# Loads of q for batch 0 are issued from ScalarE's queue instead of SyncE's

## The chip, the cores and the metric

The kernel runs on one core of one Trainium2 chip. A core has five engines that run their own instruction streams: TensorE (PE), VectorE (DVE), ScalarE (ACT), GpSimd (POOL) and SyncE (SP). In this kernel SP computes nothing and only issues transfers (DMAs). The metric is the device time of one execution in microseconds, as the median of several runs of the same program.

## What the kernel computes

Two parts follow each other for a batch of 4: a linear attention with 4 heads, 1088 positions and head size 32, and a gated feed-forward layer with a spatial (position by position) matrix. Cut to what matters:

```
a, b = S1 x, S2 x                      # 8 features each, phi(x) = all 64 products
kv = sum_s phi(k)_s v_s ;  z = sum_s phi(k)_s
attn = (phi(q) kv) / (phi(q) z + 1e-6)
h = gelu(attn @ w_in) ;  u, v = halves of h
v = layernorm(v) * g ;  v = w_sg @ v + b_sg      # w_sg is 1088 x 1088
out = attn + (u * v) @ w_out
```

## The kernel before

**Stages.** The work of batch 0's attention, the normalisation of its v and the first quarter of its spatial product are a stretch of their own, the head. From about 50 us on, a main loop runs: the spatial product of batch b on PE, and between its matmuls, small step by small step, the attention of batch b + 1. The loop's products are made of split operands (a high and a low part, the tiles with `_h` and `_l`), so each needs three matmuls.

**The head's order is written out.** `Head.build` names each step, with an engine, a length and what it comes after; a table of numbers, `HEAD`, gives each step a time, and `Steps.run` calls the steps in order of these times with the scheduler switched off. The engine that a step's entry names sorts nothing. The order in which the steps are called is the order in which each engine gets its instructions, and each engine works strictly in that order.

**The head's steps by name.** `s` is the raw projection (S1 and S2, repeated for the four heads: 128 rows, 16 KB). DVE makes `s_f` from it and from that the matrix `sk`; ACT makes eight scaled copies of `s_f`, `sab`. `k0` and `k1` load batch 0's k in two parts, 192 KB and 384 KB (128 rows of 384 and of 768 numbers). The steps `k1` on PE (line 755) multiply k by `sk` into three PSUM tiles `pk`: the first from the first part, the third and second from the other. ACT copies a piece of each, `kb` (line 764); DVE forms the features (line 146; they lie in the tile `vn`, which is named for what comes later in it). PE projects q with `sab` into `pab` (line 808), sums features times `vx` into `pkv` (line 776; `vx` is v), then forms `pnd` (numerators and denominators, line 847). DVE divides (lines 857 to 864, `den`, `xt`), PE transposes (`px`, line 873), ACT and DVE split the result into `x_h` and `x_l` (lines 876, 880). The raw weights `win_raw` are 64-bit numbers that DVE takes apart (lines 631 to 654) into `win_h`, `win_l`. The nine row blocks of the spatial matrix, `w_f`, 544 KB each, are loaded (line 707) and ACT rounds each to `w_h` (line 938).

**The loads.** `load_q(c)` loads batch 0's q in three tiles of 384 columns; the last is filled by two DMAs, as its rows end at 1088: 192, 192, 160 and 32 KB. All loads of the head are issued from SP, in this order: s, k0, k1, the four of q, the two halves of v, ident, the second half of w_in, then the blocks of `w_f` and the rest. A DMA completes on one of eight semaphores, which the program hands out in turn over all of its DMAs in the order in which their steps are called, whichever engine issues them; a DMA is not issued before the one that used the same semaphore before it has landed.

Before the head's first computed step ACT loads its table and runs one `warm` activation (line 113), and PE runs 14 small matmuls on constants (line 142).

Of the kernel before, what the change touches and what calls it, by code (L numbers as in the profile page):

```python
# [17 lines left out]
B, H, S, D, R = 4, 4, 1088, 32, 8  # L18
P = 128
NT = 9  # L20
SP = NT * P
# [67 lines left out]
def tile_kernel(ctx: ExitStack, tc: tile.TileContext, qd, kd, vd, sd, wd, bd, wind, gd, woutd, identd, outd):  # L89
    nc = tc.nc  # L90
    mm = nc.tensor.matmul
    V, A, G = nc.vector, nc.scalar, nc.gpsimd
    load = nc.sync.dma_start
# [59 lines left out]
    def spread(pool, ab, cw, name):  # L153

        d = dram.tile([2, 2, P, 3 * P], F32, tag="e", name=name + "d", bufs=3)
        load(
            d[0].rearrange("p (x j) c -> (p x) j c", j=R)[:, :, :cw],
            ab[:32, :cw].unsqueeze(1).broadcast_to([32, R, cw]),
        )
        for p in range(2):  # L160
            load(
                d[1, p].rearrange("(i x) c -> x i c", i=R)[:, :, :cw],
                ab[32 + 16 * p : 48 + 16 * p, :cw].unsqueeze(1).broadcast_to([16, R, cw]),
            )
        e = [pool([P, 2, 3 * P], "e" + x, name + x) for x in "ab"]
        for i in range(2):
            load(e[i][:, :, :cw], d[i].rearrange("p q c -> q p c")[:, :, :cw])
        return e
# [434 lines left out]
    class Head:  # L603
# [4 lines left out]
            self.pool, self.stage, self.x, self.g = pool, stage, x, g  # L608
            self.s = Steps()

        def load(self, name, ns, f, after=()):
            self.s.at(name, "SP", 0.47, f, after, late=-ns)

        def split64(self, name, hi, lo, raw, n, whole, after, late):

# [68 lines left out]
        def build(self):  # L684
# [5 lines left out]
            q = [pool([P, 512], "r", f"q0_{c}")[:, : 3 * P] for c in range(3)]  # L690
# [7 lines left out]
            def load_q(c):  # L698
                c0 = 3 * P * c
                n = min(3 * P, S - c0)  # L700
                load(q[c][:, :n], qd[0, :, c0 : c0 + n])
                if n < 3 * P:
                    load(q[c][:, n:], qd[0, :, S - (3 * P - n) : S])

            def load_w(t):
                w_f[t] = wpool([P, S], "w", f"w_f{t}")
# [3 lines left out]
            self.load("k0", 560, lambda: load(k[:, : 3 * P], kd[0, :, : 3 * P]))  # L710
            self.load("k1", 1460, lambda: load(k[:, 3 * P :], kd[0, :, 3 * P :]))
            self.load("q0", 550, lambda: load_q(0))
            self.load("q1", 550, lambda: load_q(1))
            self.load("q2", 700, lambda: load_q(2))
            self.load("v0", 760, lambda: load(vx[:, :NT], vd[0, :, 0]))
            self.load("v1", 760, lambda: load(vx[:, NT + 1 :], vd[0, :, 1]))
# [100 lines left out]
            for j in range(6):  # L817
                c, p = divmod(j, 2)
# [19 lines left out]
            n = 2 * (D + 1)  # L838
# [139 lines left out]
    late = Pool(gp, 3, gt=4)  # L978
# [114 lines left out]
```

## Time and profile before

| | us |
|---|---|
| median of 3 runs (lowest to highest) | 360.31 (360.22 to 360.52) |
| the profiled execution, its own time | 359.86 |
| its span, first to last instruction | 357.7 |
| busy: PE / DVE / ACT / POOL | 349.5 / 249.8 / 162.6 / 22.2 |
| the head, until the main loop's first matmul (line 390) | 0 to 50.42 |

The profile is that of one execution, 0.45 us below the median of the runs; 2.2 us of its time lie outside the span. A row of the timeline gives start, duration, engine, line, operation, output and inputs; in brackets the idle time of the engine ahead of it and what ended it. PE's durations overlap each other, since matmuls are pipelined; the distance between starts is what counts there. Where PE or DVE shows no bracket, it followed its previous instruction at once. For a DMA, the issue on the queue (SPq, ACTq) and the time from issue to landing are shown apart. TensorE's granted clock is 0.998 over the run.

### The profile page before, as it was taken

The page shows a single profiled execution, that of the slowest core. Times are in us where ns is not written, and L with a number is a line of the kernel's source. Part 1 is how long each engine was busy: PE and PEld are TensorE (multiplying, and loading weights), DVE is VectorE, ACT ScalarE, POOL GpSimd, SP SyncE. Part 2 cuts the span into 40 slices and gives each one's busy share as a digit, 9 for nine tenths or more (in the row PEclk, how much of TensorE's full clock was granted, in tenths as well). Part 3 has the DMA queues.
Part 4 walks back from the last instruction along what each step waited for, and adds up shares of the span by engine and source line. Part 5 has one row for each costly group of instructions (what it writes and reads, how often), then busy time and mean ns, then how long its engine had stood idle before and what let it go on. Part 6 is the DMA issues. An engine that isn't in the chain of part 4 may idle for free.

```text
span 357.7 us, 5455 instructions
## 1 busy us (share of the span) xinstructions
PE 349.5 (98%) x2024; PEld 321.2 (90%) x2024; DVE 249.8 (70%) x606; ACT 162.6 (45%) x355; POOL 22.2 (6%) x37
## 2 busy tenths in 40 slices
PE   8999999999999999999999999999999999999995
PEld 7876679998989999999898999999998899999994
DVE  5797899967999767627859765663696948642333
ACT  5475942325553963214546682332445595231210
POOL 0003000103010000022020000020202000000000
PEclk9999999999999999999999999999999999999999
DMA  7993005853400044483000007683000000100001
GB/s 227 394 412 134 2 0 98 237 174 66 123 21 2 0 103 128 149 222 138 2 0 23 1 0 160 132 206 88 2 0 1 2 0 23 41 0 2 0 2 62
DMA packets 18265, 30.18 MB, mean 84 GB/s; under 512 B 1984, under 2 KB 15168, under 8 KB 18240
## 3 DMA queue, kind: packets, MB, share of 16 engines
q1 hardware_dynamic: 18096, 29.77, 28.6%
q8 instruction: 16, 0.26, 0.3%
q10 hardware_dynamic: 144, 0.08, 0.1%
q14 instruction: 9, 0.07, 0.1%
HBM read 20.92 MB, written 8.91 MB: 83 GB/s over the span
## 4 chain that ended last, share of the span: by engine, by line
PE 82%; DVE 5%; ACT 5%; DMA 4%; POOL 1%; SPq 1%; issue 1%; DVEq 0%
PE pz L373 18%; PE pz L381 18%; PE pz L375 16%; PE pkv L202 3%; DMA w_f<-in_w 3%; ACT vn L345 2%; PE pu L390 2%; PE pz L932 2%; PE pv L297 2%; PE po L460 2%; PE pu L391 2%; PE pu L392 2%; PE po L458 2%; PE pv L298 2%; PE po L459 2%; PE pv L299 2%
## 5 line engine op out<-in xcount | busy, mean ns | idle before, releaser
L373 PE MATMUL pz<-w_h,vh 128*128 128x362 f32 (+3 forms) x405 | 133.6, 332 | 0.2 <-ACT vh L358 0.2
L381 PE MATMUL pz<-w_l,vh 128*128 128x362 f32 (+3 forms) x405 | 129.5, 329 | 0.0
L375 PE MATMUL pz<-w_h,vl 128*128 128x364 f32 (+3 forms) x360 | 118.2, 328 | 0.0
L373 PEld LDWEIGHTS pz<-w_h,vh 128*128 128x128 f32 x405 | 75.9, 188 | 2.0 <-ACT vh L358 1.0
L381 PEld LDWEIGHTS pz<-w_l,vh 128*128 128x128 f32 x405 | 75.5, 188 | 0.4
L375 PEld LDWEIGHTS pz<-w_h,vl 128*128 128x128 f32 x360 | 67.7, 188 | 1.2 <-DVE vl L363 0.4
L402 DVE SCALAR_TENSOR_TENSOR gt<-pz,g_col,b_bc 128x362 f32<-128x362 f32 (+3 forms) x47 | 27.5, 591 | 37.3 <-PE pz L381 36.8
L428 ACT CAST gh<-gt 128x362 fp32r<-128x362 f32 (+3 forms) x47 | 23.1, 497 | 57.9 <-PE po L459 47.6
L395 ACT ACTIVATE u<-pu 128x362 f32<-128x362 f32 (+3 forms) x48 | 22.6, 473 | 28.7 <-PE pu L392 27.3
L429 DVE TENSOR_TENSOR gl<-gt,gh 128x362 fp32r<-128x362 f32 (+3 forms) x47 | 24.6, 531 | 15.6 <-ACT gh L428 15.1
L345 ACT ACTIVATE vn<-vn,nm,rs 128x512 f32<-128x512 f32 x36 | 27.4, 811 | 6.3 <-POOL nm L679 3.9
L363 DVE TENSOR_TENSOR vl<-vn,vh 128x384 fp32r<-128x384 f32 (+2 forms) x60 | 23.0, 420 | 9.1 <-ACT vh L358 8.9
L425 DVE TENSOR_TENSOR gt<-gt,u 128x362 f32<-128x362 f32 (+3 forms) x47 | 25.2, 544 | 3.9 <-ACT u L395 3.5
L268 DVE RECIPROCAL den<-den 128x362 f32<-128x362 f32 (+1 forms) x9 | 21.8, 2417 | 8.7 <-ACT den L265 8.7
L358 ACT CAST vh<-vn 128x384 fp32r<-128x384 f32 (+1 forms) x63 | 23.0, 419 | 5.4 <-PE pz L381 5.4
L302 ACT ACTIVATE vn<-pv 128x512 f32<-128x512 f32 x27 | 15.9, 600 | 12.4 <-PE pv L299 12.1
L932 PE MATMUL pz<-w_f,vn 128*128 128x362 f32 (+3 forms) x54 | 18.0, 476 | 0.8 <-ACT vn L345 0.7
L305 DVE BATCH_NORM_STATS2 st<-vn 128x6 f32<-128x512 f32 x27 | 17.8, 676 | 0.6 <-ACT vn L302 0.5
L390 PE MATMUL pu<-x_h,win_h 128*128 128x362 f32 (+3 forms) x48 | 17.0, 354 | 0.2 <-ACT u L395 0.2
L460 PE MATMUL po<-gl,wout_h 128*128 128x362 f32 (+3 forms) x47 | 15.8, 336 | 0.9 <-DVE gl L429 0.9
L932 PEld LDWEIGHTS pz<-w_f,vn 128*128 128x128 f32 (+1 forms) x54 | 9.8, 189 | 7.6 <-ACT vn L345 2.4
L146 DVE TENSOR_TENSOR kp<-pk,kb 128x256 f32<-128x256 f32 x27 | 11.3, 422 | 7.1 <-ACT kb L190 4.4
(198 smaller groups left out, 525.6 us busy)
## 6 DMA issues: line engine op xcount, KB each, us to landing
w_f<-in_w SPq DMA_DIRECT2D x9, 544.0 KB, 9.8
vx<-in_v SPq DMA_DIRECT2D x8, 288.0 KB, 5.4
k<-in_k SPq DMA_DIRECT2D x3, 576.0 KB, 5.5
e_0d<-ab SPq DMA_DIRECT2D x3, 364.0 KB, 4.2
e_0d<-ab SPq DMA_DIRECT2D x6, 182.0 KB, 5.4
e_0a<-e_0d SPq DMA_DIRECT2D x3, 364.0 KB, 4.0
e_0b<-e_0d SPq DMA_DIRECT2D x3, 364.0 KB, 4.1
q<-in_q SPq DMA_DIRECT2D x6, 181.0 KB, 2.4
```

Of the source, the lines that this page charges most:

```text
L345: A.activation(self.vn[:, t], self.vn[:, t], AF.Identity, bias=self.nm[:, t : t + 1], scale=self.rs[:, t : t + 1])
L358: A.copy(vh[:, ts], vs[:, ts])
L363: self.last = V.tensor_sub(vl[:, ts], vs[:, ts], f32(vh[:, ts]))
L373: last = mm(z, lhsT=vh[:, t], rhs=w_h[:, t, cs], start=(t == 0), stop=False)
L375: last = mm(z, lhsT=vl[:, t], rhs=w_h[:, t, cs], start=False, stop=False)
L381: mm(z, lhsT=self.parts[db][0][:, t], rhs=w_l[t][:, c0 : c0 + cw], start=False, stop=(t == NT - 1))
L390: mm(pu, lhsT=win_h[:, ws], rhs=xh[:, cs], start=True, stop=False)
L402: V.scalar_tensor_tensor(gt, z, g_col[:, db : db + 1], b_bc[:, c0 : c0 + cw], op0=ALU.mult, op1=ALU.add)
L425: V.tensor_mul(gt, gt, u)
L428: A.copy(gh, gt)
L429: V.tensor_sub(gl, gt, f32(gh))
L932: return mm(zs[ci], lhsT=g.vn[r, t, :P], rhs=w_f[t][r, c0 : c0 + cw], start=(t == 0), stop=(t == NT - 1),)
```

## The change

`load_q` of the head issues its DMAs through `A.dma_start` (ACT's queue), where it used `load`, which is `nc.sync.dma_start`. `Head.load` gets an argument for the engine that a step's entry names; no call passes it.

```
-        def load(self, name, ns, f, after=()):
-            self.s.at(name, "SP", 0.47, f, after, late=-ns)
+        def load(self, name, ns, f, after=(), eng="SP"):
+            self.s.at(name, eng, 0.47, f, after, late=-ns)
...
             def load_q(c):
                 c0 = 3 * P * c
                 n = min(3 * P, S - c0)
-                load(q[c][:, :n], qd[0, :, c0 : c0 + n])
+                A.dma_start(q[c][:, :n], qd[0, :, c0 : c0 + n])
                 if n < 3 * P:
-                    load(q[c][:, n:], qd[0, :, S - (3 * P - n) : S])
+                    A.dma_start(q[c][:, n:], qd[0, :, S - (3 * P - n) : S])
```

The loads of q for batches 1 to 3 (line 223) stay on SP. Neither PE, DVE nor POOL gets another order of instructions. On ACT's queue at the start of the program, before:

```order
L113 ACT_TABLE_LOAD
L113 ACTIVATE warm<-eps_t 128x1 [waits DVE_49]
L743 ACTIVATE sab<-s_f,mask_67 128x8x8 [waits DVE_49]
L743 ACTIVATE sab<-s_f,mask_67 128x8x8 x4
L734 CAST sk_h<-sk 128x128 [waits DVE_49,Pool_49]
```

and now:

```order
L701 DMA q_0_138<-in_q 128x384
L113 ACT_TABLE_LOAD
L113 ACTIVATE warm<-eps_t 128x1 [waits DVE_49]
L701 DMA q_1_139<-in_q 128x384
L701 DMA q_2_140<-in_q 128x320
L703 DMA q_2_140<-in_q 128x64
L743 ACTIVATE sab<-s_f,mask_67 128x8x8 [waits DVE_49]
L743 ACTIVATE sab<-s_f,mask_67 128x8x8 x4
L734 CAST sk_h<-sk 128x128 [waits DVE_49,Pool_49]
```

The first load of q now stands ahead of ACT's table load, the other three between `warm` and `sab`. None of them waits. On SP's queue at the start, before:

```order
L709 DMA s_raw<-in_s 128x16
L710 DMA k_137<-in_k 128x384
L711 DMA k_137<-in_k 128x768
L701 DMA q_0_138<-in_q 128x384
L701 DMA q_1_139<-in_q 128x384
L701 DMA q_2_140<-in_q 128x320
L703 DMA q_2_140<-in_q 128x64
L715 DMA vx<-in_v 128x576
L716 DMA vx<-in_v 128x576 [waits DMAHW0_49]
L717 DMA ident<-in_ident 128x192 [waits DMAHW1_49]
L718 DMA win_raw_134<-in_w_in 128x512 [waits DMAHW2_49]
L707 DMA w_f_165<-in_w 128x1088 [waits DMAHW3_49]
```

and now:

```order
L709 DMA s_raw<-in_s 128x16
L710 DMA k_137<-in_k 128x384
L711 DMA k_137<-in_k 128x768
L715 DMA vx<-in_v 128x576
L716 DMA vx<-in_v 128x576 [waits DMAHW0_49]
L717 DMA ident<-in_ident 128x192 [waits DMAHW1_49]
L718 DMA win_raw_134<-in_w_in 128x512 [waits DMAHW2_49]
L707 DMA w_f_165<-in_w 128x1088 [waits DMAHW3_49]
```

All that stood behind q moves up by four issues. The waits carry the same names, but semaphore 0 is now that of q's first tile, 1 that of s, 2 and 3 those of k's two parts, 4 that of q's second tile, 5 that of the first half of v, 6 and 7 those of q's third: so the second half of v waits for q's first tile to land (before: for s), ident for s, `win_raw` for k's first part and the first `w_f` for its second.

## The prediction

> **What bounds the kernel now.** I read the page's table of engines first, then the chain that ended last, then the timeline of the first 21 us, then the transfers of that time in steps of half a microsecond.
>
> ```profile
> PE 349.5 (98%) x2024; PEld 321.2 (90%) x2024; DVE 249.8 (70%) x606; ACT 162.6 (45%) x355; POOL 22.2 (6%) x37
> 0.00:50.42 50.42, 48.19 (x241) 34.25 (x242) 39.69 (x123) 33.43 (x60) 3.58 (x18) 1.00 0.56 207
> 50.42:357.70 307.28, 301.29 (x1784) 286.95 (x1783) 210.16 (x484) 129.22 (x295) 18.63 (x19) 1.00 0.25 64
> ```
>
> The two lower rows are the busy times of PE, weight loads, DVE, ACT and POOL in the head and in the rest, then the clock, the DMA engines' share and GB/s. From 50.42 us on PE is busy 301.29 of 307.28 us, and nothing in that part is changed. So the change is worth what it moves the head's end, microsecond for microsecond. Of the head's chain the part that bears on the loads is this:
>
> ```profile
> 4.00 5.06 DMA vx<-in_v
> 9.08 9.77 DMA w_f<-in_w
> 18.87 1.10 ACT w_h L938
> 19.97 0.38 ACT x_h L876
> ```
>
> It says: v landed at 9.06, that freed the semaphore for a block of `w_f`, the block landed at 18.87, and ACT's rounding of it held up `x_h`. Taken alone this promises time for anything that brings v and `w_f` forward. But a chain shows one of several that may be almost as long, so I look at the engines beside it:
>
> ```profile
> 4.43 2.54 PE L755 MATMUL pk<-sk,k 128*128 128x128 f32 x18 [0.25 <-PE warm L142]
> 5.36 1.41 PEld L755 LDWEIGHTS pk<-sk,k 128*128 128x128 f32 x12 [0.21 <-PE pk L755]
> 6.81 3.39 PE L808 MATMUL pab<-q,sab 128*128 128x384 f32 x10
> 10.04 4.18 PE L776 MATMUL pkv<-vx,vn 128*128 128x128 f32 x36
> 16.83 0.17 DVE L857 TENSOR_SCALAR den<-pnd 128x12 f32<-128x12 f32 x1 [0.33 <-PE pnd L847]
> 19.56 0.69 DVE L654 TENSOR_TENSOR win_l<-wi1t,wi1e 128x512 fp32r<-128x512 f32 x1
> 20.38 0.56 DVE L880 TENSOR_TENSOR x_l<-px,x_h 128x384 fp32r<-128x384 f32 x1
> 5.36:16.83 11.47, 11.44 (x75) 9.61 (x76) 8.25 (x23) 5.64 (x15) 0.00 (x0) 1.00 1.01 364
> 16.83:30.97 14.14, 13.79 (x67) 9.41 (x66) 13.14 (x41) 10.57 (x17) 0.86 (x5) 1.00 0.95 375
> ```
>
> PE works without a gap from 5.36 to the `pnd` for which DVE waits at 16.83 (11.44 of 11.47 us busy), and the products, `pab` and `pkv` among them, follow each other with no bracket. From 16.83 DVE takes over (13.14 of 14.14 us). The chain by the loads joins that second run only at 20.38: DVE is done with `win_l` at 20.25 and starts `x_l` at 20.38. Without the late `w_f`, `x_l` could start 0.13 us sooner and no more. That is all that earlier v and `w_f` can give.
>
> The start of PE's gapless run is what counts then, and its ends are two loads:
>
> ```profile
> s_raw<-in_s SPq DMA_DIRECT2D x1, 16.0 KB, 1.8
> k<-in_k SPq DMA_DIRECT2D x1, 192.0 KB, 2.4
> k<-in_k SPq DMA_DIRECT2D x1, 384.0 KB, 3.6
> 0.73 0.38 SPq L709 DMA_DIRECT2D s_raw<-in_s  x1
> 1.17 0.42 SPq L710 DMA_DIRECT2D k<-in_k  x1
> 1.63 0.43 SPq L711 DMA_DIRECT2D k<-in_k  x1
> 2.53 0.17 DVE L631 TENSOR_SCALAR st<-s_raw 128x16 int32<-128x16 int32 x1 [1.24 <-DMA s_raw<-in_s]
> 3.98 0.18 DVE L728 TENSOR_TENSOR sk<-s_f,mask 128x32 f32<-128x32 f32 x1
> ```
>
> s lands at 0.73 + 1.8 = 2.53, DVE's ten small operations end at 4.16, PE starts `pk` at 4.43. k's second part lands at 1.63 + 3.6 = 5.23, and PE, which by its pace of 0.11 us a matmul would have gone on at about 5.1, goes on at 5.36. So k's second part ends the last wait ahead of PE's run; s has some 0.25 us to spare, k's first part (3.57) 0.8 us.
>
> **What the change does to the loads.** q's first tile is now issued at about 0.72 beside s, ahead of both parts of k; the other three come after `warm`, while k's second part is under way. The transfers in half microseconds (the last two numbers are the DMA engines' share and GB/s):
>
> ```profile
> 1.50:2.00 0.50, 0.50 (x8) 0.50 (x7) 0.00 (x0) 0.50 (x1) 0.00 (x0) 1.00 0.21 32
> 2.00:2.50 0.50, 0.50 (x8) 0.50 (x7) 0.00 (x0) 0.21 (x2) 0.00 (x0) 1.00 0.49 90
> 2.50:3.00 0.50, 0.50 (x7) 0.50 (x6) 0.44 (x3) 0.00 (x0) 0.00 (x0) 1.00 1.15 289
> 3.50:4.00 0.50, 0.50 (x7) 0.49 (x5) 0.43 (x4) 0.13 (x1) 0.00 (x0) 1.00 0.84 301
> 4.50:5.00 0.50, 0.50 (x5) 0.50 (x6) 0.00 (x0) 0.50 (x3) 0.00 (x0) 1.00 1.01 360
> DMA packets 49, 0.15 MB, mean 301 GB/s; under 512 B 0, under 2 KB 0, under 8 KB 49
> DMA packets 128, 0.18 MB, mean 360 GB/s; under 512 B 15, under 2 KB 124, under 8 KB 128
> ```
>
> The last two rows are the packets of 3.5 to 4.0 (k's second part, 3 KB each, one row of the tile) and of 4.5 to 5.0 (nearly all of q).
>
> *q's first tile.* It has 128 packets like those of the last row, which take the engines about 0.5 us. Between 1.5 and 2.5 they are idle for 0.5 x 0.79 + 0.5 x 0.51 = 0.65 us. If the tile comes as early as s did, nearly all of it fits there: lower bound 0. If it misses that gap, k's second part lands 0.5 us later: upper bound. I take 0.05, nearer to the gap, as s with the same issue time had its packets there.
>
> *q's second and third tile.* ACT issues them one after another from 2.67 (below). k's second part had its first packets about 1.5 us after its issue, so these come at about 4.0 and meet what is then left of it, some 80 of its 128 packets (49 had gone in the window to 4.0). If the engines serve the two queues packet by packet, 80 packets of q at 0.5 us for 128 stand between: 0.3 us. If k's queue goes first, 0; if q's goes first with all three, 0.38 MB at 360 GB/s is 1.05 us. I take 0.3, by the packets seen in the rows. The Trainium skill (DMA: Bandwidth & Descriptors, Queues, rings and completion order) has each engine change queues only after a whole packet, typically 9 to 17 descriptors; by that the eight rows that an engine holds of k would pass in one piece, this 0.3 would be 0, and the sum below would be 0.3 us less. The trace counts one packet for each row (0.15 MB in 49), which fits the 0.3 better.
>
> *s.* Its packets and those of q's first tile come together. Row against row, s is late by at most the tile's 0.5 us, of which 0.25 is spare; lower bound 0, since the engines had gaps all through its time. I take 0.2, inside the spare time: nothing is added, as PE waits for k anyway.
>
> *SP's issues.* Four issues at 0.47 us a piece fall away there, so that v stands 1.88 us earlier in the queue. The engines are full from 2.5 us on, so the data behind comes sooner only by what q put into the early gap, up to 0.5 us. The second half of v now waits for q's first tile, which lands at about 3; ident for s, `win_raw` for k's first part, the first `w_f` for its second, at about 5.6 (before, it was issued at 5.90). None of these is late against a backlog that lasts to 29 us. What this gives is bounded by the 0.13 us above; I take all of it. Where that goes, `win_l` on DVE is what `x_l` waits for next.
>
> *ACT's issues.* The queue's own price stands at the end of the run, and at the start ACT runs this:
>
> ```profile
> 354.40 0.37 ACTq L456 DMA_DIRECT2D out<-o  x1
> 2.02 0.20 ACT L113 ACTIVATE warm<-eps_t 128x1 f32<-128x1 f32 x1
> 3.87 1.31 ACT L743 ACTIVATE sab<-s_f,mask 128x64 f32<-128x64 f32 x5 [1.65 <-DVE s_f L646]
> 5.39 0.24 ACT L764 COPY kb<-pk 128x96 f32<-128x96 f32 x1
> 6.34 0.24 ACT L764 COPY kb<-pk 128x96 f32<-128x96 f32 x1 [0.71 <-PE pk L755]
> ```
>
> At 0.37 (this row) to 0.47 (SP's spacing) one issue moves `warm` from 2.02 to about 2.45, its end to 2.65, and three more end at 3.8 to 4.1. `sab` has to start at 3.87, so it is late by 0 to 0.2 us; behind it stand `sk_h` and the first `kb`, and then 0.71 us in which ACT waits for PE. That gap covers the 0.2 at no cost. Were it gone, DVE's features would start late by as much.
>
> **The sum.** PE's run starts later by 0.05 + 0.3 = 0.35 us. It is gapless to 16.83 and DVE's is nearly so behind it, so the delay arrives at 20.25 whole; there 0.13 comes back. The head ends 0.22 us later. On the profiled execution's 359.86 that is 360.08, on the median 360.31 it is 360.53; I say 360.5.
>
> **The rivals.** *It is hidden, or gives a little.* q's tile fits into the idle 0.65 us and k's rows are not held up, as the packet rule above would have it; then 0.13 us comes back and no more: 360.2, with 360.15 to 360.35 as its range. For it speaks the share of 0.21 and 0.49 before 2.5 us; against it the full engines from then on. *Slower by more than can be called the same.* All of q goes ahead of k's second part: 0.5 for the first tile and at least 0.5 of the others' 1.05, so k lands over 1 us late and the time is 360.31 + 1.0 - 0.13 = 361.2; up to 361.7. It decides from a landing at 5.23 + 0.72 + 0.13 = 6.1 us on. For it speaks that k's packets are the slow ones (301 GB/s where q ran at 360); against it that two queues are fed at once and k's is issued before q's second tile. *Clearly faster.* The chain is right at face value: ACT's wait ahead of the late block,
>
> ```profile
> 18.87 1.10 ACT L938 CAST w_h<-w_f 128x1088 fp32r<-128x1088 f32 x1 [0.97 <-DMA w_f<-in_w]
> ```
>
> 0.97 us, is all on the path, and the four issues saved ahead of v remove it: 359.35. Against it stands `win_l`'s end at 20.25. *The change does not do what it says:* excluded, as the DMAs stand on ACT's queue ahead of `sab` without a wait.
>
> **Chances and range.** The forecast (later by 0.05 to 0.65 us, 360.35 to 360.95) has 0.60, hidden 0.22, slower 0.13, clearly faster 0.05. By runs that spread over 0.3 us, 0.2% or 0.7 us is what can be told from no change here. Under 359.6 there is then 0.05, over 361.0 there is 0.13, and 0.82 lies between. The range goes from the hidden case's lower end, 360.1, to the slower one's price, 361.2; outside lie the faster case and half of the slower one.
>
> **What would show it.** The profile of the changed kernel should have q's first tile landing at 2.7 to 3.3, k's second part at 5.4 to 5.8 (before 5.23), the first matmul on it at 5.5 to 5.9 (before 5.36), `den` at about 17.2 (before 16.83), `x_l` without a wait for `x_h`, and the main loop's first `pu` (line 390) at about 50.65 (before 50.42). If k lands at 5.25 or sooner, the terms of q are wrong; if it lands late and `den` does not move, PE's run has slack that I did not see; if `den` moves and 50.42 does not, the slack is in DVE's run. A `pu` sooner than 50.2 would mean that I misjudged the path by the loads.

## The result and the profile after

The changed kernel is slower: 364.32 us median of 4 runs (363.65 to 364.62), against 360.26 us (359.78 to 360.52) for the kernel before on the same chip. The ratio is 1.0101, interval 1.0069 to 1.0133. The profiled execution took 364.49 us with a span of 362.5, which is 4.8 more than before. The forecast was 360.5, its range ended at 361.2.

The page's table of engines and the busy times of the head and of the rest (PE, weight loads, DVE, ACT, POOL; then clock, DMA share, GB/s):

```profile
PE 351.7 (97%) x2024; PEld 323.4 (89%) x2024; DVE 249.8 (69%) x606; ACT 162.6 (45%) x355; POOL 22.3 (6%) x37
0.00:55.17 55.17, 50.46 (x241) 36.36 (x241) 39.70 (x123) 33.64 (x60) 3.60 (x18) 1.00 0.51 189
55.17:362.50 307.33, 301.27 (x1784) 287.00 (x1783) 210.15 (x484) 128.92 (x295) 18.67 (x19) 1.00 0.25 64
```

The main loop takes what it took (307.33 us, before 307.28). All of the difference lies in the head, which ends 4.75 us later. PE is busy 2.27 us longer there (50.46 against 48.19) with the same 241 matmuls. So there are two losses: PE waits longer, and the same matmuls take longer. Of the 2.27 us about 0.7 are the first six `pk`, which only fill the wait for k; the rest, 1.59, is worked out below.

The start of the timeline (start, duration, engine and line):

```profile
0.73 0.40 ACTq L701 DMA_DIRECT2D q<-in_q  x1
0.73 0.38 SPq L709 DMA_DIRECT2D s_raw<-in_s  x1
1.16 1.28 ACT L113 ACT_TABLE_LOAD   x1 [1.16 <-PEq L1079]
1.17 0.42 SPq L710 DMA_DIRECT2D k<-in_k  x1
1.22 0.88 ACTq L701 DMA_DIRECT2D q<-in_q  x2
1.63 0.43 SPq L711 DMA_DIRECT2D k<-in_k  x1
2.12 0.45 ACTq L703 DMA_DIRECT2D q<-in_q  x1
2.45 0.20 ACT L113 ACTIVATE warm<-eps_t 128x1 f32<-128x1 f32 x1
3.10 0.18 DVE L631 TENSOR_SCALAR st<-s_raw 128x16 int32<-128x16 int32 x1 [1.80 <-DMA s_raw<-in_s]
```

The issues of the same time, in KB each and us from issue to landing:

```profile
s_raw<-in_s SPq DMA_DIRECT2D x1, 16.0 KB, 2.3
q<-in_q ACTq DMA_DIRECT2D x2, 192.0 KB, 2.9
k<-in_k SPq DMA_DIRECT2D x1, 192.0 KB, 3.0
k<-in_k SPq DMA_DIRECT2D x1, 384.0 KB, 6.8
```

q's second and third tile are issued at 1.22 and 1.64, although they stand behind the table load and `warm` in ACT's order, and `warm` does not run before 2.45. ACT's queue hands out a DMA that waits for nothing while the engine is still at work on what stands ahead. So at 1.7 us both of q's first two tiles (384 KB) are with the DMA engines, ahead of k's second part or beside it. s takes 2.3 us to land (before 1.8), k's first part 3.0 (2.4), its second part 6.8 (3.6): it lands at 8.47 where it landed at 5.26 (5.23 by the rounded numbers of the prediction).

The packets of the two queues (q10 is ACT's, q1 SP's) in the four half microseconds from 2.0 to 4.0 us, in packets, MB and share of the 16 engines:

```profile
q10 hardware_dynamic: 52, 0.08, 43.3%
q1 hardware_dynamic: 81, 0.01, 12.4%
...
q10 hardware_dynamic: 84, 0.10, 57.0%
q1 hardware_dynamic: 67, 0.07, 46.1%
...
q1 hardware_dynamic: 74, 0.11, 60.5%
q10 hardware_dynamic: 48, 0.07, 39.0%
...
q10 hardware_dynamic: 91, 0.12, 64.1%
q1 hardware_dynamic: 38, 0.06, 43.9%
```

Some 0.37 of the 0.62 MB are q's, in a time in which before nothing but s and k was under way.

Then PE and DVE in the head:

```profile
5.00 1.62 PE L755 MATMUL pk<-sk,k 128*128 128x128 f32 x6 [0.81 <-DVE sk L728]
8.57 0.71 PEld L755 LDWEIGHTS pk<-sk,k 128*128 128x128 f32 x3 [2.25 <-issue]
8.61 2.90 PE L755 MATMUL pk<-sk,k 128*128 128x128 f32 x12 [1.99 <-DMA k<-in_k]
11.30 3.71 PE L808 MATMUL pab<-q,sab 128*128 128x384 f32 x10
14.84 4.18 PE L776 MATMUL pkv<-vx,vn 128*128 128x128 f32 x36
21.64 0.17 DVE L857 TENSOR_SCALAR den<-pnd 128x12 f32<-128x12 f32 x1 [0.32 <-PE pnd L847]
24.97 0.55 DVE L880 TENSOR_TENSOR x_l<-px,x_h 128x384 fp32r<-128x384 f32 x1
55.17 0.43 PE L390 MATMUL pu<-x_h,win_h 128*128 128x364 f32 x1
```

The busy times from the twelve `pk` of k's second part to the first `pab`, and from the same start to `den`:

```profile
8.61:11.30 2.69, 2.69 (x13) 2.69 (x13) 0.77 (x3) 0.96 (x4) 0.00 (x0) 1.00 0.77 232
8.61:21.64 13.03, 13.03 (x75) 11.00 (x76) 7.84 (x23) 5.57 (x13) 0.00 (x0) 1.00 0.97 378
```

The first of these stretches in the kernel before:

```profile
5.36:6.81 1.45, 1.42 (x13) 1.45 (x13) 0.62 (x2) 0.73 (x5) 0.00 (x0) 1.00 1.07 344
```

The weights of k's second part go in at 8.57, before at 5.36: 3.21 us later, by the wait. Thirteen matmuls then need 2.69 us where they needed 1.45, at a granted clock that the column gives as 1.00 in both. With the first `pab` the way from there to `pkv` takes 6.27 us against 4.68 (14.84 - 8.57, 10.04 - 5.36): 1.59 us of slower pace. 3.21 + 1.59 = 4.80, which is `pkv`'s delay, and `den` is 4.81 late (21.64 against 16.83). PE is busy 13.03 of 13.03 us from 8.61 to there, so nothing of it is made good.

### The profile page after: what moved, and what is told of

The parts are those of the page before. It is cut to its first block, busy times and chain, and to the rows that moved or that the text cites. A ratio compares the mean times of both kernels' runs of the same rounds, so it can differ in the third digit from the quotient of the medians.

```text
span 362.5 us, 5455 instructions
## 1 busy us (share of the span) xinstructions
PE 351.7 (97%) x2024; PEld 323.4 (89%) x2024; DVE 249.8 (69%) x606; ACT 162.6 (45%) x355; POOL 22.3 (6%) x37
## 4 chain that ended last, share of the span: by engine, by line
PE 86%; DVE 5%; ACT 4%; DMA 2%; POOL 1%; issue 1%; SPq 0%; DVEq 0%
PE pz L373 18%; PE pz L381 18%; PE pz L375 16%; PE pkv L202 3%; ACT vn L345 2%; PE pu L390 2%; PE pz L932 2%; PE pv L297 2%; PE po L460 2%; PE pu L391 2%; PE pu L392 2%; DMA k<-in_k 2%; PE pab L808 2%; PE po L458 2%; PE pv L298 2%; PE po L459 2%
```

## The experiments

Each was timed beside the kernel before on the same chip: 360.01 us in the first group of four kernels, 360.21 in the second four, 359.93 in the third group, 360.11 in the last. Edits are against the changed kernel, unless it says before.

**1. Only q's first tile on ACT's queue, the other three loads with SyncE's.**

```
-                A.dma_start(q[c][:, :n], qd[0, :, c0 : c0 + n])
+                start = load if c else A.dma_start
+                start(q[c][:, :n], qd[0, :, c0 : c0 + n])
...
```

> Only q's first tile goes out on ScalarE's queue; the other three loads of q stay on SyncE's behind k. In the changed kernel k's second part landed at 8.47 us instead of 5.26, 3.2 us later, and 4.06 us were lost. Theory (bytes): k is late by the bytes of q served ahead of it or beside it, here 192 of the 576 KB, so it lands about 1.0 us late, at 6.0 to 6.5; the loss is about 1 us plus what TensorE's slow start costs: 361.0 to 362.0. Rival (queue): two queues being served side by side cost by themselves, whatever the bytes; then k lands at 8 or later and the time is 363.5 to 364.5. Rival (v): k is held by v, which was issued 1.9 us sooner; here v moves by only 0.5 us, so 360.3 to 360.8.

Measured: 362.00 us (360.87 to 362.66, 10 runs), ratio 1.0041 (1.0020 to 1.0062). Its timeline:

```profile
3.05 0.17 DVE L631 TENSOR_SCALAR st<-s_raw 128x16 int32<-128x16 int32 x1 [1.75 <-DMA s_raw<-in_s]
4.94 4.27 PE L756 MATMUL pk<-sk,k 128*128 128x128 f32 x18 [0.76 <-DVE sk L729]
9.00 3.46 PE L809 MATMUL pab<-q,sab 128*128 128x384 f32 x10
```

s is late by 0.52 us from this tile alone. k's second part landed at 6.17, but its 18 `pk` follow each other without a wait; they take 4.06 us to the first `pab`, where the kernel before took 2.38 with a wait in it. So here the loss is s's delay (`pk` starts at 4.94, before at 4.43) and the pace (1.68 us); k lands as the bytes had it, but PE does not wait for it. The runs fall into two groups, three near 360.9 and seven from 361.9 to 362.7.

**2. The opposite: q's second and third tile on ACT's queue, the first with SyncE's.**

```
-                A.dma_start(q[c][:, :n], qd[0, :, c0 : c0 + n])
+                start = A.dma_start if c else load
+                start(q[c][:, :n], qd[0, :, c0 : c0 + n])
...
```

> The opposite split: q's first tile is issued by SyncE behind k as before, the second and third (384 KB) by ScalarE from the start. Bytes: k's second part lands about 2 us late, at 7.0 to 7.5, and the time is 362.0 to 363.5; with the run of the first tile alone the losses add up to that of the whole change. Queue: 363.5 to 364.5. v: it is issued 1.4 us sooner, so about three quarters of the 4 us, 363.0 to 363.5, with k late only once v's packets run.

Measured: 362.12 us (360.83 to 362.41, 10 runs), ratio 1.0044 (1.0027 to 1.0061). s landed at 2.85, k's second part at 6.47, and PE's row for it reads:

```profile
6.60 2.79 PE L756 MATMUL pk<-sk,k 128*128 128x128 f32 x12 [0.22 <-DMA k<-in_k]
```

k landed sooner than the 7.0 to 7.5 expected. Either part of q ahead of k is enough to lose 2 us. The two losses add up to that of the whole change in number (1.99 + 2.11 = 4.10 against 4.06), but not in kind: each has the slow pace in it, which the whole change pays once, and with both parts ahead k is later and PE waits besides.

**3. One queue only: all loads with SyncE, but q's first two tiles ahead of k's second part.** Against the kernel before; in the order table the entries of k's second part and of q's first two tiles change.

```
-    0, 0.252, 0.94, 1.41, 1.88, 2.35, ...
+    0, 0.252, 1.9, 0.94, 1.41, 2.35, ...
```

> Everything stays on SyncE's queue; the first two tiles of q (384 KB) are issued ahead of k's second part, so that k is issued 0.95 us later. Bytes: k lands behind 384 KB more at the rate of the slowest DMA engine, 1.5 to 2 us late (6.7 to 7.3), and the time is 362.0 to 363.5, like the split with 384 KB on ScalarE. Queue: without a second queue k is late only by the two tiles at the mean rate or by its issue, 1.0 us, and lands at 6.2: 361.0 to 361.5. v: it keeps its issue time, so k is not held by it: 361.0 to 361.3.

Measured: 363.66 us (363.41 to 364.04, 4 runs), ratio 1.0087 (1.0053 to 1.0120). Its timeline has the two loads of q at 1.63 and k's second part at 2.58, and then:

```profile
4.38 0.91 PE L755 MATMUL pk<-sk,k 128*128 128x128 f32 x6 [0.20 <-PE warm L142]
7.50 2.76 PE L755 MATMUL pk<-sk,k 128*128 128x128 f32 x12 [2.22 <-DMA k<-in_k]
```

k's second part landed at 7.37, a little behind the expected range, and so does the time. Without any second queue the loss is nearly that of the change. It is the order in which bytes reach the DMA engines that costs. (The way is not quite the same: k is also issued 0.95 us later here, and from there takes 4.8 us to land where it took 3.6 before and 6.8 in the change.) s is early here (2.48) and the first six `pk` run at 0.91 us; after 2.22 us of waiting the next twelve run at half pace all the same.

**4. The second queue, but later.** A copy on ACT that reads s stands ahead of q's loads, so that ACT issues them when s has landed.

```
+                if c == 0:
+                    A.copy(stage([P, 1], "seen", "s_seen"), raw_s.bitcast(I32)[:, :1])
                 A.dma_start(q[c][:, :n], qd[0, :, c0 : c0 + n])
```

> The changed kernel, but ScalarE first copies one element of s, so that its queue waits for s to land (2.5 us) before it issues q's four loads at 2.6 to 4.3 us. q still goes by ScalarE's queue, v is still 1.9 us earlier on SyncE's. Bytes: s and k are ahead again, s lands at 2.5 and k's second part at 5.3 to 5.9; TensorE's gap stays at 0.25 us; 360.0 to 361.0. Queue (two queues side by side cost by themselves): k at 6.5 or later, 361.5 to 364. v (the early v holds k): k at 6 or later as well, 361.5 to 363.

Measured: 360.86 us (359.81 to 362.27, 8 runs), ratio 1.0015 (0.9995 to 1.0034): not told from no change. Its timeline:

```profile
2.49 1.38 ACTq L703 DMA_DIRECT2D q<-in_q  x3
4.38 2.43 PE L757 MATMUL pk<-sk,k 128*128 128x128 f32 x18 [0.35 <-DVE sk L730]
8.04 3.46 PE L810 MATMUL pab<-q,sab 128*128 128x384 f32 x10 [1.23 <-DMA q<-in_q]
```

q is issued from 2.49 on, as the prediction had it for the second tile. s and k's second part then land at 2.46 and 5.10, and `pk` runs as before. What is left is a wait for q itself, which now comes behind k and v. The first half of v is issued at 2.10 here as in the changed kernel, and does k no harm.

**5. Fewer bytes.** The same queue, issue times and rows, but only the first quarter of the columns of each tile is loaded; GpSimd fills the rest with a constant.

```
-                A.dma_start(q[c][:, :n], qd[0, :, c0 : c0 + n])
+                m = n // 4
+                A.dma_start(q[c][:, :m], qd[0, :, c0 : c0 + m])
+                G.memset(q[c][:, m:n], 0.5)
...
```

> The changed kernel with a quarter of q's bytes: the same four loads on ScalarE's queue at the same times and with the same number of rows, but a quarter of each row; GpSimd fills the rest with a constant. Its output is not the reference's, it loads 144 KB of q instead of 576. Bytes: k's second part is late by about a quarter, 0.8 us, s by 0.1 to 0.3, and the gap on TensorE is near 0.5 us: 360.3 to 362.0. Queue or number of rows: the same rows alternate with k's rows, so k is as late as in the changed kernel, 363.5 to 364.5.

Measured: 359.71 us (359.41 to 361.49, 10 runs), ratio 0.9994 (0.9976 to 1.0012). s landed at 2.52, k's second part at 5.81, and in the profiled execution PE kept its pace (three of the ten runs lie at 361.2 to 361.5, the others at 359.4 to 359.8):

```profile
4.83 0.91 PE L758 MATMUL pk<-sk,k 128*128 128x128 f32 x6 [0.75 <-DMA k<-in_k]
5.94 1.58 PE L758 MATMUL pk<-sk,k 128*128 128x128 f32 x12 [0.20 <-DMA k<-in_k]
```

Together with 3 and 4 this settles what the first loss hangs on: q's bytes ahead of s and k, neither the queue nor the number of rows. How these bytes cost as much as they do is another question (below).

**6. The pace by itself.** The kernel before, with 10 small matmuls ahead of the head's first product instead of 14; no load is touched.

```
-WARM = 14
+WARM = 10
```

> The kernel before, unchanged in its loads, with 10 instead of 14 small matmuls at the start: TensorE is idle for about 1.2 us ahead of the first k product instead of 0.25. Theory (the gap costs by itself): the k products run at half their pace, 18 matmuls at 0.1 us more each, and the time is 361.5 to 362.3 though every load lands as before. Rival (the slow pace comes with the late loads): no change, 359.8 to 360.5.

Measured: 361.51 us (361.21 to 362.46, 4 runs), ratio 1.0043 (1.0027 to 1.0059). The loads land as before (s 2.34, k's second part 5.41), but:

```profile
4.28 4.18 PE L755 MATMUL pk<-sk,k 128*128 128x128 f32 x18 [0.96 <-DVE sk L728]
8.25 3.52 PE L808 MATMUL pab<-q,sab 128*128 128x384 f32 x10
51.94 0.44 PE L390 MATMUL pu<-x_h,win_h 128*128 128x364 f32 x1
```

From `pk` to `pab` it takes 3.97 us (before 2.38), and the main loop starts 1.52 late. Four small matmuls fewer and so a gap of 0.96 us on PE, with no load late, costs as much as the second loss.

**7. The changed kernel with PE kept at work.** 18 small matmuls at the start, and 14 more between the first six and the other twelve `pk`.

```
-WARM = 14
+WARM = 18
...
             def k1(c):
+                if c == 2:
+                    keep = bank("keep", "po2", 1)[:64, :64]
+                    for i in range(14):
+                        mm(keep, lhsT=vx[:, NT], rhs=vx[:, NT], start=True, stop=True)
```

> The changed kernel with TensorE kept at work on constants in its two idle gaps: 18 instead of 14 small matmuls at the start, and 14 more between the first and the second k product. In the changed kernel the 18 matmuls of the k products were spaced by some 0.21 us after the gaps (0.11 in the kernel before), and the stretch from the second k product to the features' product took 6.23 us instead of 4.65. Theory (two parts): k's second part lands some 3 us late, and TensorE, having been idle for over 0.5 us, then works at half its pace for a while, which costs another 1.6 us. Then this kernel gets those 1.6 us back, k as late as before: 362.3 to 363.0. Rival: the slow matmuls are slow because their operands or the transfers beside them are, not because of the gap; then the time stays at 364.0 to 364.6.

Measured: 362.54 us (362.10 to 362.61, 4 runs), ratio 1.0064 (1.0049 to 1.0079). PE's rows:

```profile
0.93 4.10 PE L142 MATMUL warm<-vx 128*64 128x64 f32 x36 [0.93 <-POOL vx L124]
4.97 1.60 PE L759 MATMUL pk<-sk,k 128*128 128x128 f32 x6
6.50 1.84 PE L756 MATMUL keep<-vx 128*64 128x64 f32 x28
8.28 1.60 PE L759 MATMUL pk<-sk,k 128*128 128x128 f32 x12
```

k's second part landed at 7.88, late as ever, but the twelve `pk` behind it take 1.60 us in place of 2.90. Against the changed kernel's 364.32 some 1.8 us come back, though the two were not timed side by side; 1.3 of it is the twelve `pk`, and about 0.6 that k lands sooner here than at 8.47. The first six `pk` are slow without any gap ahead of them; so it is not the gap by itself that decides. The same small matmul (one of the 18 is two instructions in the row) takes 4.10 / 36 = 0.114 us in the first row and 1.84 / 28 = 0.066 us in the third.

**8. v held back.** Four 16-byte loads go ahead of v, so that the semaphores make v wait for k.

```
+            def load_v0():
+                for i in range(4):
+                    load(pad[:, 4 * i : 4 * i + 4], gd[:1])
+                load(vx[:, :NT], vd[0, :, 0])
...
```

> The changed kernel, but with four loads of 16 bytes ahead of v on SyncE's queue, by which v's first half waits until k's second part has landed and everything behind it is later too. v: k then lands at about 5.3 to 5.8. Bytes and queue: k lands at 7.5 to 8.5 as in the changed kernel, since v stands behind k on the same queue. The time itself is not to tell much: v comes late here, at k's landing plus about 3 us, so 362 to 366 under either.

Measured: 362.16 us (360.90 to 362.39, 10 runs), ratio 1.0048 (1.0032 to 1.0065), k's second part at 6.68, which is neither forecast. Taken alone this would mean that v, which in the changed kernel follows k at once, makes up the difference to 8.47. But the changed kernel was not run beside it, so both were run once more on one chip:

> The changed kernel once more, for a second look at when k's second part lands: 8.47 us in its first profile and 7.88 in the run with TensorE kept at work, which has the same loads. If the delay of 2.6 to 3.2 us is of the order of the loads, it lands at 7.3 to 8.7 again and the time is 363.5 to 364.7; if the first look was a rare one, at 6.3 to 7.0 and 362 to 363.

> The kernel with v held until k has landed once more: k's second part landed at 6.68 us there, 1.8 us sooner than in the changed kernel. If v's early bytes add to k's delay, it lands at 6.3 to 7.0 again; if that look was a lucky one, at 7.3 to 8.5.

The changed kernel gave 361.88 us there, with v held back 361.28. PE's rows for k's second part, first of the changed kernel:

```profile
4.94 1.62 PE L755 MATMUL pk<-sk,k 128*128 128x128 f32 x6 [0.76 <-DVE sk L728]
6.81 2.38 PE L755 MATMUL pk<-sk,k 128*128 128x128 f32 x12 [0.25 <-DMA k<-in_k]
```

and with v held back:

```profile
4.82 1.62 PE L762 MATMUL pk<-sk,k 128*128 128x128 f32 x6 [0.64 <-DVE sk L735]
6.79 2.32 PE L762 MATMUL pk<-sk,k 128*128 128x128 f32 x12 [0.35 <-DMA k<-in_k]
```

k lands at 6.67 and 6.65. On this chip v makes no difference, and in experiments 4 and 5 it was as early and k at 5.10 and 5.81. How late k is differs from occasion to occasion: with v early it landed at 6.67, 7.88 (experiment 7), 8.08 (experiment 9) and 8.47, with v held at 6.65 and 6.68. One pair on one chip does not exclude that v has a share in the later ones.

**9. The changed kernel timed again, on another chip.**

> The changed kernel timed once more, on whatever chip it falls: its first four runs took 363.65 to 364.62 us with k's second part at 8.47 us, a later single run 361.88 with k at 6.67. If the part of the delay beyond q's bytes (24 rows of q for each DMA engine at 0.065 us, 1.5 us) is a matter of single stalled rows that differ from run to run, the runs spread from about 361 to 364.6 with a median near 362.5, k lands anywhere from 6.5 to 8.5. If the first four were the rule, the median is 364 again.

Measured: 364.77 us (364.67 to 365.00, 4 runs), ratio 1.0132 (1.0115 to 1.0148). k's second part landed at 8.08.

```profile
8.21 2.90 PE L755 MATMUL pk<-sk,k 128*128 128x128 f32 x12 [1.60 <-DMA k<-in_k]
```

I had expected a wide spread about 362.5, and that was a miss: on this chip four runs agree within 0.33 us, at the first result's level. The one execution at 361.88 stands apart from the eight timed runs at 363.65 to 365.00, and whether that is the chip or the occasion these runs don't tell.

**10. The kernel before with 16 small matmuls at the start.** Does it close the 0.25 us gap ahead of `pk` with a gain?

```
-WARM = 14
+WARM = 16
```

> The kernel before with 16 instead of 14 small matmuls at the start, so that TensorE has hardly a gap (4.64 against 4.43 us) ahead of the first k product, which starts 0.2 us later but in time for k's second part at 5.3. Theory (half pace after a gap, in some executions of the kernel before too): of its 42 runs five took 361 to 362.5 us, the others 359.6 to 360.6; those five vanish, the median stays: 359.7 to 360.3, none over 360.8. Rival: the slow runs have another cause, and one in eight stays over 361.

Measured: 360.16 us (359.54 to 360.68, 12 runs), ratio 1.0002 (0.9990 to 1.0014). No gain in the median, so no version that beats the kernel before was found. None of its runs is over 361, while 5 of the 59 of the kernel before in the first three groups are (361.22 to 362.47). That would fit a head that now and then runs its first products at half pace, but it shows little: at 5 in 59, twelve runs have none about one time in three, and no profile shows such a run. Nor does closing the gap alone give the fast pace: in the profile here no gap stands ahead of `pk` (4.53 to 7.24), yet its 18 take 2.71 us, against 2.38 before with a wait in it.

## Why the prediction was wrong

Three things failed: the time at which q's second and third tile are issued, the size of the terms for q (0.35 us together, where k's second part came 3.21 us late), and PE's pace, which stood nowhere in the sum (1.59 us).

**ACT's issue times.** The prediction had q's second and third tile issued "one after another from 2.67", when `warm` had ended. They were issued at 1.22 and 1.64. The order of instructions was read as an order in time; but the two loads wait for nothing, and the queue of ACT works ahead of the engine. Where a real wait holds all of q until 2.49 (experiment 4), k's second part lands at 5.10, no later than before, and the time can't be told from before; what is left there is PE's wait for q, which was not in the forecast. But the issue times alone do not explain the miss: in experiment 1 the second and third tile stay behind k, and q's first tile alone costs 1.99 us.

**The terms "q's first tile" (0.05) and "q's second and third tile" (0.3).** The first was taken to fit into the engines' idle time; in experiment 1 the tile by itself put s 0.52 and k's second part 0.91 us later. The second was sized for a k that is half served when most of q arrives. In fact 384 KB of q stood ahead of it or beside it. At the 360 GB/s of the prediction's row these take 1.05 us, and all 576 KB 1.6. By my own reading of the trace, the landing of a transfer is the last of 16 completions, one for each DMA engine: for k's second part they ran from 4.64 to 5.26 before, with 4.81 in the middle, and from 5.14 to 8.47 after, with 5.88 in the middle. The middle is late by 1.07, and by 1.2 to 1.6 in the three other profiles with the same loads (experiments 7, 8 and 9), as the bytes have it. The other 2.1 us of the landing are spread between the engines: before, the last is 0.45 behind the middle, after, 2.59. In the changed kernel one 3 KB row of k, begun at 5.12, took 1.80 us where the median row takes 0.12; seven more rows of k follow it one by one from 6.91 on, and their engine is 1.33 behind the last but one. Such rows are in the trace of before too, the longest from 6.3 us on, when k was through and v was hit. Whether k met them because it was late, or q made them more, no run here tells apart, and it stays open. It sets whether the change costs some 2 us (k at 6.67) or over 4 (8.08 and 8.47).

**The packet rule** that the prediction weighed against the 0.3 does not hold here, and the prediction was right to go by single rows. When the other DMA engines are through with k's second part, one has seven rows of it left: they start at 6.91, 7.08, 7.25, 7.42, 7.59, 7.76 and 7.93 and take 0.12 us each, and in every gap between them stands one row of q's third tile (1280 bytes, 0.055 us, at 7.03, 7.20, 7.37, 7.54, 7.71 and 7.88). So this engine takes a row from either queue in turn; its rows of k do not pass in one piece.

**"s ... inside the spare time: nothing is added".** s landed at 3.1, 0.57 late where up to 0.5 was allowed and 0.2 taken, against a spare time of 0.25. That alone would have been covered by the wait for k. What was not in the sum is that the products behind may run at half pace when PE starts late (it idles 0.81 us ahead of `pk`). This term was missing, and it measured 1.59 us here, and in experiment 6, by itself, 1.59 to `pab` and 1.52 at the main loop. It is most of the loss in experiment 1.

**What held.** PE's run is gapless up to `den` and hands the delay on whole: 4.80 at `pkv`, 4.81 at `den`. The waits by v and `w_f` were worth as little as was said: `x_l` starts 4.59 late, 0.21 less (0.13 was said), of which 0.05 is left at the main loop's first `pu`. q's first tile landed at 3.3, the end of its range. ACT's issues delayed `warm` to 2.45 as worked out and cost nothing. SyncE's four issues saved gave nothing to be seen.

**The rivals.** "Slower by more than can be called the same" was the right one, with most of its mechanism: two tiles of q go ahead of k's second part and the third beside it, and it lands behind the 6.1 us from which it decides. It got 0.13 of the chance, since two queues were taken to be served in turn, which they are, and k to be issued ahead of q's second tile, which it was not. Its price, 361.2 to 361.7, was the bytes alone; it lacked the pace and the spread between the engines.

## What to carry to other kernels

At the start of a kernel the order in which bytes are handed to the DMA engines is the schedule of the loads: moving a load to an idle queue frees no DMA engine, but lets it overtake what the first products wait for. Where a load stands behind computing instructions on its queue, take its issue for as early as its own waits allow, unless the trace shows otherwise; and if it has to come later, make it wait for something. A late operand ahead of TensorE's first products can cost more than the delay, since the products behind the gap may run at half pace.

## What the runs showed of the hardware

**A queue runs ahead of its engine.** DMAs behind ACT's table load (1.16 to 2.44) and `warm` (2.45) were issued at 1.22, 1.64 and 2.12. The Trainium skill (DMA: Bandwidth & Descriptors, Issuing engines are not separate DMA queues) says that loads from several engines run on the same 16 DMA engines and interleave, and that a second issuer saves only the issuing time. The packet counts of the two queues agree, and experiment 3 shows that the second queue is not needed for the loss; what the saved issuing time did here was to put q ahead, at a cost of 4 us.

**TensorE's pace at the start.** The same matmul of 128 by 128 takes 0.11 or 0.21 us, and the granted clock reads 1.00 in both. In experiment 7 the first small matmuls take 0.114 us, later ones 0.066, so the head begins at the slow pace. The kernel before does too (28 in 3.25 us, 0.116 each), but runs its `pk` from 4.43 on at the fast one. Experiment 3 shows the way back: its first six `pk` are fast, and behind 2.22 us of waiting the next twelve are slow. The rows do not give a length of gap that decides: 0.76 (experiment 1), 0.81, 0.96 and 2.22 us were followed by slow products, 0.75 (experiment 5) and 1.23 (experiment 4) by fast ones, and the first `pk` of experiments 7 and 10 were slow without one. What sets the moment at which the pace changes stays open. The Trainium skill (TensorE: Matmul & The Clock Gate, Part 1: The HAM clock gate) has the array start at half rate and change by how busy it was in a window of about 3.4 us that runs on its own, whatever the kernel does. The two paces, and groups of runs 1 to 2 us apart as in experiments 1 and 5, agree with that; the window itself is in no trace here. For the middle of a kernel the Trainium skill (TensorE: Matmul & The Clock Gate, Why this matters for your kernels) asks to avoid gaps over about 3 us; at the start of this head that is no licence for shorter ones: with a gap of 0.96 us and four small matmuls fewer (experiment 6) it lost 1.5 us.
